# One attention and expert kernel: the product with v as 64-row products only, router work in smaller groups and other places, constants on another queue

## The chip, the cores and the metric

The kernel runs on one core of a Trainium2 chip. The metric is the device time of one execution in microseconds (us); lower is better. A profiled execution also leaves a trace, in which every instruction has its engine, its start and its length. The engines are PE (TensorE: matmuls; its weight loads are listed apart as PEld), DVE (VectorE), ACT (ScalarE), POOL (GpSimd) and SP (SyncE, which here only issues transfers). Each engine works through its own instructions in order.

## The reference

Two parts follow each other. The first is attention over a sliding window of 64 keys, for 8 batches, 8 heads, 576 positions and a head size of 64. The second routes each of the 4608 resulting rows of 512 numbers: a row whose skip score is not positive is left as it is, any other row goes through the one expert (of 8) with the highest logit and gets the weighted result added.

```python
scores = np.where(mask, scale * np.matmul(q, k.transpose(0, 1, 3, 2)), -1e9)   # mask: 0 <= rel < 64
attn = np.exp(scores - np.max(scores, axis=-1, keepdims=True))
attn = attn / (np.sum(attn, axis=-1, keepdims=True) + 1e-09)
x = np.matmul(attn, v)                       # then rows of 8 heads x 64 = 512
do_compute = x @ w_skip > 0
e_idx = np.argmax(xc @ w_gate, axis=1)       # xc: the rows that compute
h = np.maximum(xc[mask] @ w1[e], 0.0)
y[mask] = gate_w[mask, None] * (h @ w2[e])
out[do_compute] = xc + y
```

All data are float32.

## The kernel before

**Tiles.** The rows are cut into blocks of 64 positions, and two blocks make a token tile of 128 rows; there are 36 tiles, 0 to 35. Since the window is 64 wide, a block needs its own keys ("now") and those of the block before it. In most tiles the two blocks follow each other in one batch, so the keys and values of the first block are also the "before" block of the second. Tiles 8, 17, 26 and 35 are tail tiles: they hold the ninth blocks of two batches and share nothing. In tiles 0, 4, 9, 13, 18, 22, 27 and 31 the first block opens a batch and has no block before it.

**The attention loop.** The instructions are issued in a written-out order. Iteration t of the loop does this: `score(t + 1)` multiplies q with k on PE (16 matmuls into `ps`); the gate step of this tile, if there is one, on PE and ACT (`gate` multiplies vT with the router weights into `pw`, copied to `vw`; `gate_t` turns that round into `pk`, copied into nine extra columns of `vm`, so that the product with v yields the router's logits too); `transpose_p(t)` transposes the softmax numerators `s` on PE into `pt`, and ACT copies (`pm`) and POOL and DVE multiply with a mask to give `ptm`; `soften(t + 1)` takes the masked scores (DVE, `ps`), the maximum (DVE, `mx`), and the exponentials (ACT, `nmx` and eight instructions into `s`); `tile_out(t - 1)` calls `av_tile`, which multiplies `ptm` with v on PE into `av` and lets DVE divide by the row sums (`r`, `x`, `lh`).

**The product with v.** `av_tile` has two forms. In a tail tile every product has 64 rows of keys and 64 columns of queries: for each of four head pairs q, two windows, two blocks and two heads z. In the other tiles the block that both need is multiplied once for both, with 128 query columns (the part `(0, 2, 1, ...)` of the list `parts`), and the two other products have 64 columns. The trace has two records for each such matmul.

**The buffers.** `pt`, `pw` and `pk` take turns in two PSUM buffers (tag "t"); `ps` has two; `av` has one.

**The router.** `GRP` cuts the tiles into groups; when the last tile of a group is done, the generator `route` is queued, and `routes(1)` runs one step of it (a step is up to a `yield`) on DVE. Its matmuls (`sums`) go into the free end of `av`. Each row then gets a place in an expert's list, and POOL writes the list entries with indirect transfers, one per tile (`scatter`), which `pace` issues one or two at a time. After tile 21 (`NCLOSE` = 22 tiles) the two fullest experts are found (`close_first`), their lists are read back (`first_lists`), and their rows fetched (`gather_x`, indirect transfers `xg<-out,es`), so that the first expert can start while the last tiles are worked on. `split` transposes these rows on PE (`px`) in the iterations of `XSPLIT`; `U0` are the iterations in which SP issues the first six weight loads (`raw`), `USPLIT` that of the first split of weights. For 17 < t < 30 (set by `TWICE`) ACT and POOL do half of `ptm` and DVE the other half; otherwise ACT and POOL do three quarters. From iteration `TWICE` on two scatters are issued per iteration.

**The experts.** When the tiles are done, PE works through the experts' matmuls in `float32r` halves (`p`, `yw`, `yv`, `yu`), for which ACT and DVE split each weight piece in two (`whi`, `wlo`).

**Transfers.** q, k, vT, vm and the stores of x are issued by SP in order, and each new transfer on SP or ACT waits until the eighth before it has landed. They are spread over the tiles by `feed`, four or five tiles ahead of their use. The constants are issued by ACT; `load_constants` (the router's tables and the emptying of the lists) stands at the end of the opening loads.

## Time and profile before

| | before |
|---|---|
| median of 3 runs | 497.98 us (493.5 to 498.54) |
| the profiled execution | 500.87 us, of which the span from first to last instruction is 499.2 us |
| PE, DVE, ACT, POOL busy | 451.2, 283.0, 211.3, 178.5 us |
| mean granted TensorE clock | 0.934 |
| attention on PE (first to last product with v) | 20.0 to 231.9 us |

The page of the profile gives the busy time of each engine over the whole span and, in 40 slices, its share in tenths. [...] The chain of waits is followed back from the last instruction: at each step it names what released the work, so its rows in the attention show which engine set the pace there.

### The profile page before, as it was taken

To read this page: it belongs to the slowest core of one execution; us is meant where nothing else is said; L and a number is where in the kernel's file an instruction comes from. 1 tells how busy PE (TensorE), PEld (TensorE's weight loads), DVE (VectorE), ACT (ScalarE), POOL (GpSimd) and SP (SyncE) were. 2 spreads that over 40 slices of the span, in tenths; PEclk is the share of its full clock that TensorE was granted. 3 is DMA by queue.
4 is the path that set the end of the run, shared out by engine and by line. 5 is a ranking of instruction groups with operands and counts; after the bars stand their busy time and mean duration, and the time that the engine had idled before them with its cause. 6 is when DMAs were issued, how large, how long until landed. Compare 5 with 4: busy or idle time off the path is not lost.

```text
span 499.2 us, 12731 instructions
## 1 busy us (share of the span) xinstructions
PE 451.2 (90%) x5001; PEld 365.7 (73%) x5001; DVE 283.0 (57%) x600; ACT 211.3 (42%) x604; POOL 178.5 (36%) x213
## 2 busy tenths in 40 slices
PE   3999999899988994988798999999999999999990
PEld 3677767666765773767797988898888889888770
DVE  2356665665666664457963364967437456666420
ACT  1665665444434452334731252443424435543410
POOL 4343443344644546336525351420604313101010
PEclk9999999898977897668899999999999999999996
DMA  8879998868877698316743455364645655656000
GB/s 306 334 226 298 301 298 256 313 176 275 224 257 213 181 356 301 110 44 201 260 121 142 165 186 167 121 245 149 205 161 173 204 180 183 224 194 207 3 26 18
DMA packets 34958, 99.90 MB, mean 200 GB/s; under 512 B 6092, under 2 KB 7910, under 8 KB 34888
## 3 DMA queue, kind: packets, MB, share of 16 engines
q1 hardware_dynamic: 28864, 88.52, 54.5%
q0 software_dynamic: 4864, 9.90, 5.9%
q8 instruction: 40, 0.66, 0.5%
q10 hardware_dynamic: 1168, 0.65, 0.4%
q14 instruction: 22, 0.18, 0.1%
HBM read 84.82 MB, written 14.94 MB: 200 GB/s over the span
## 4 chain that ended last, share of the span: by engine, by line
PE 76%; DVE 8%; DMA 6%; issue 3%; ACT 3%; another core or an unknown queue 0%; POOLq 0%; SPq 0%; ACTq 0%; DVEq 0%
PE av L376 17%; PE p L750 7%; PE p L751 7%; PE p L752 7%; PE ps L244 5%; PE pt L276 5%; PE yw L750 3%; PE yv L750 3%; PE yw L751 3%; PE yv L751 3%; PE yw L752 3%; PE yv L752 3%; DMA raw<-wq 3%; PE px L739 2%; PE pk L339 2%
## 5 line engine op out<-in xcount | busy, mean ns | idle before, releaser
L376 PE MATMUL av<-vm,ptm 64*64 64x74 f32 (+1 forms) x1536 | 101.5, 285 | 1.9 <-DVE lh L394 1.5
L703 DVE TENSOR_TENSOR wlo<-raw,whi 128x1024 fp32r<-128x1024 f32 x72 | 87.8, 1222 | 14.3 <-ACT whi L702 12.4
L376 PEld LDWEIGHTS av<-vm,ptm 64*64 64x64 f32 (+1 forms) x1536 | 75.2, 164 | 27.6 <-issue 9.3
L787 ACT ACTIVATE hh<-p 128x256 fp32r<-128x256 f32 (+6 forms) x72 | 27.7, 385 | 140.6 <-PE p L752 139.2
L750 PE MATMUL p<-xh,whi 128*128 128x256 f32 (+6 forms) x288 | 85.8, 298 | 1.1 <-DVE hl L788 1.1
L751 PE MATMUL p<-xl,whi 128*128 128x256 f32 (+6 forms) x288 | 84.7, 294 | 0.0
L752 PE MATMUL p<-xh,wlo 128*128 128x256 f32 (+6 forms) x288 | 84.5, 293 | 0.0
L702 ACT CAST whi<-raw 128x1024 fp32r<-128x1024 f32 x72 | 74.5, 1046 | 0.0
L284 POOL TENSOR_TENSOR ptm<-pm,mask 128x512 f32<-128x512 f32 x36 | 45.9, 1276 | 76.1 <-ACT pm L283 76.0
L788 DVE SCALAR_TENSOR_TENSOR hl<-p,hh 128x256 fp32r<-128x256 f32 (+6 forms) x72 | 30.3, 420 | 70.3 <-ACT hh L787 64.6
L267 ACT ACTIVATE s<-ps,nmx 128x64 f32<-128x64 f32 x288 | 63.0, 330 | 1.2
L810 POOL DMA_INDIRECT out<-yo,les x18 | 19.0, 1054 | 122.3 <-DVE yo L809 109.8
L750 PEld LDWEIGHTS p<-xh,whi 128*128 128x128 f32 x288 | 55.7, 193 | 4.0 <-DVE hl L788 1.2
L528 POOL DMA_INDIRECT lists<-ent,gdi x36 | 40.7, 1130 | 46.4 <-DVE lh L394 22.6
L751 PEld LDWEIGHTS p<-xl,whi 128*128 128x128 f32 x288 | 55.8, 194 | 1.4
L752 PEld LDWEIGHTS p<-xh,wlo 128*128 128x128 f32 x288 | 55.7, 194 | 0.0
L276 PE MATMUL pt<-ident,s 128*128 128x128 f32 x144 | 34.5, 328 | 13.1 <-ACT vw L328 6.3
L386 DVE TENSOR_SCALAR r<-av 128x8 f32<-128x8 f32 x36 | 6.0, 166 | 71.1 <-PE av L376 69.4
L244 PE MATMUL ps<-k,q 64*64 64x128 f32 (+1 forms) x1024 | 42.7, 295 | 0.8 <-issue 0.8
L276 PEld LDWEIGHTS pt<-ident,s 128*128 128x128 f32 x144 | 16.3, 153 | 30.7 <-ACT vw L328 11.3
L244 PEld LDWEIGHTS ps<-k,q 64*64 64x64 f32 x1024 | 34.8, 153 | 2.0 <-issue 1.8
L750 PE MATMUL yw<-whi,hh 128*128 128x512 f32 x80 | 32.3, 403 | 0.0
(171 smaller groups left out, 703.2 us busy)
## 6 DMA issues: line engine op xcount, KB each, us to landing
raw<-wq SPq DMA_DIRECT2D x72, 512.0 KB
vm<-vp SPq DMA_DIRECT2D x16, 592.0 KB
vT<-vT SPq DMA_DIRECT2D x16, 512.0 KB
out<-x SPq DMA_DIRECT2D x32, 256.0 KB
q<-qT SPq DMA_DIRECT2D x14, 512.0 KB
k<-kT SPq DMA_DIRECT2D x7, 640.0 KB
k<-kT SPq DMA_DIRECT2D x7, 512.0 KB
kt<-kT SPq DMA_DIRECT2D x8, 256.0 KB
```

What stands on the lines that cost most here:

```text
L244: nc.tensor.matmul(ps[64 * hf : 64 * hf + 64, z, p, 64 * w.start :], q[h, p], k[h, w, p], start=True, stop=True, skip_group_check=True,)
L267: nc.scalar.activation(s[:, q, z], cur[:, z, q], AF.Exp, bias=nmx[:, z, q : q + 1], scale=0.125)
L276: nc.tensor.transpose(pt[:, i], s[:, 2 * g + i].rearrange("p z c -> p (z c)"), ident)
L284: nc.gpsimd.tensor_tensor(part(0, 2), split(pm[:, 0:2], 2), kept(2), op=ALU.mult)
L376: nc.tensor.matmul(av[64 * f0 : 64 * f1, z, q * VW : (q + 1) * VW], ptm[h, q, j : j + f1 - f0], v[h, q], start=first, stop=not first or (f ...
L528: ins = nc.gpsimd.indirect_dma_start(out=lists, out_offset=bass.IndirectOffsetOnAxis(ap=di, axis=0), in_=ent.bitcast(I32), in_offset=None, ...
L702: nc.scalar.copy(hi, raw)
L703: nc.vector.tensor_tensor(lo, raw, hi.bitcast(F32), op=ALU.subtract)
L750: nc.tensor.matmul(o, lh, rh, start=first, stop=False)
L751: nc.tensor.matmul(o, lh, rl, start=False, stop=False)
L752: nc.tensor.matmul(o, ll, rh, start=False, stop=last)
L788: beat(nc.vector.scalar_tensor_tensor(hl[:, f], p1, 0.0, hh[:, f].bitcast(F32), op0=ALU.max, op1=ALU.subtract))
```

## The change

- `av_tile` has one form for all tiles, that of the tail tiles: for each head pair and window, 64 by 64 products of the two blocks and two heads. The 128-column product is gone; a full tile takes 32 matmuls in place of 24, a tile that opens a batch 24 in place of 16.
- The gate steps come after `transpose_p(t)` and no longer before it.
- The router groups are 8, 8, 6, 8, 4, 2 tiles in place of 14, 8, 8, 4, 2; the boundary at tile 22 stays.
- The three calls of `routes` per iteration stand after `soften` and the loads, after `masks`, and at the end. The first stood ahead of `soften`.
- `load_constants` is issued by SP in iteration 1; on ACT the order of the small constants differs, and an exponential of the tile of ones (scale 0) is run there ahead of the first softmax.
- `U0`, `USPLIT`, `XSPLIT` and `TWICE` are one iteration later.

```diff
-U0 = (28, 29, 30, 31, 32, 33)
-USPLIT = (34,)
+U0 = (29, 30, 31, 32, 33, 34)
+USPLIT = (35,)
-XSPLIT = (32, 33)
+XSPLIT = (33, 34)
-TWICE = 20
+TWICE = 21
...
     def load_constants():
-        nc.scalar.dma_start(cf, a["c_f"])
-        nc.scalar.dma_start(trib, a["c_tri"])
-        nc.scalar.dma_start(
+        nc.sync.dma_start(cf, a["c_f"])
+        nc.sync.dma_start(trib, a["c_tri"])
+        nc.sync.dma_start(
...
-        nc.gpsimd.memset(onesb, 1.0)
...
-        shared = win[0][0] is win[1][1]
         for q in range(4):
-            parts = [] if shared else [(hf, hf + 1, 2 * hf + 1, win[hf][0], True) for hf in range(2)]
-            if shared:
-                parts.append((0, 2, 1, win[0][0], True))
-            parts += [
-                (0, 1, 0, win[0][1], False),
-                (1, 2, 3 if shared else 2, win[1][0] if shared else win[1][1], False),
-            ]
...
+            for w in range(2):
+                for hf in range(2):
+                    if win[hf][w] is None:
+                        continue
+                    for z in range(2):
+                        h = slice(64 * z, 64 * z + 64)
+                        nc.tensor.matmul(
+                            av[64 * hf : 64 * hf + 64, z, q * VW : (q + 1) * VW],
+                            ptm[h, q, 2 * hf + 1 - w],
+                            win[hf][w][h, q],
...
-    GRP = [14, 8, 8, 4, 2]
+    GRP = [8, 8, 6, 8, 4, 2]
...
         load_qk(0, 0, 2)
+        nc.scalar.dma_start(band, a["c_band"])
         nc.scalar.dma_start(identb, a["c_identb"])
-        nc.scalar.dma_start(band, a["c_band"])
         nc.scalar.dma_start(sel, a["c_sel"])
+        nc.scalar.dma_start(wg, a["wg"])
         nc.scalar.dma_start(ident, a["c_ident"])
         nc.scalar.dma_start(mask, a["c_mask"])
-        nc.scalar.dma_start(wg, a["wg"])
+        nc.gpsimd.memset(onesb, 1.0)
+        nc.scalar.activation(onesb, onesb, AF.Exp, scale=0.0)
...
-        load_constants()
...
             score(t + 1)
+            masks = transpose_p(t)
             for f, n in gate_at.get(t, ()):
                 f(n)
-            masks = transpose_p(t)
             rest = its[0].split(*xhl[0], XSPLIT.index(t), "t") if t in XSPLIT else None
-            routes(1)
             soften(t + 1)
             pace(1)
             feed(t, 0)
+            if t == 1:
+                load_constants()
+            routes(1)
             masks()
+            routes(1)
...
-            routes(1)
             routes(1 if t < NCLOSE - 1 else 2)
```

In iteration 5 PE's order before is this (`ps` are the scores of tile 6, `pk` a gate step, `pt` the transposes of tile 5, `av` the product of tile 4 or 5 with v; the line numbers of the changed kernel are up to 8 lower):

```order
L244 MATMUL ps<-k_109,q 64x128 x16
L339 MATMUL pk<-ident,vw_470 64x64 x8
L276 MATMUL pt<-ident,s 128x128 x4
L376 MATMUL av<-vm,ptm 128x74 x2
L376 MATMUL av<-vm,ptm 64x74 x4
L376 MATMUL av<-vm,ptm 128x74 x2
L376 MATMUL av<-vm,ptm 64x74 x4
L376 MATMUL av<-vm,ptm 128x74 x2
L376 MATMUL av<-vm,ptm 64x74 x4
L376 MATMUL av<-vm,ptm 128x74 x2
L376 MATMUL av<-vm,ptm 64x74 x4
```

and now this:

```order
L243 MATMUL ps<-k_109,q 64x128 x16
L275 MATMUL pt<-ident,s 128x128 x4
L338 MATMUL pk<-ident,vw_499 64x64 x8
L368 MATMUL av<-vm,ptm 64x74 x32
L243 MATMUL ps<-k_110,q 64x128 x16
L275 MATMUL pt<-ident,s 128x128 x4
```

The gate step has moved behind the transposes, and 24 products of two widths have become 32 of one.

At the same place ACT's order (the copies of the gate step and of the transposes, then the exponentials of the next tile) was

```order
L328 COPY vw_470<-pw 128x256
L283 COPY pm<-pt 128x256
L287 COPY pm<-pt 128x128
L264 ACTIVATE nmx<-mx 128x8
L267 ACTIVATE s<-ps,nmx 128x64 x8
```

and is

```order
L282 COPY pm<-pt 128x256
L286 COPY pm<-pt 128x128
L327 COPY vw_499<-pw 128x256
L263 ACTIVATE nmx<-mx 128x8
L266 ACTIVATE s<-ps,nmx 128x64 x8
```

The copy of the gate step now stands between the copies of the transposes and the exponentials.

On DVE the first router group began, before, like this (`lg` to `gfm` are router steps, `ps` and `mx` the next tile's softmax, `ptm` the masks):

```order
L394 TENSOR_TENSOR lh<-av,r 128x8x9
L421 TENSOR_REDUCE lg<-lh 128x126
L428 TENSOR_REDUCE gmx<-lg 128x14
L430 TENSOR_TENSOR gd<-lg,gmx 128x112
L433 SCALAR_TENSOR_TENSOR gfi<-gd,cf 128x112
L435 TENSOR_REDUCE gfm<-gfi 128x14
L260 COPY_PREDICATED ps<-sel,ps 128x8x64
L263 TENSOR_REDUCE mx<-ps 128x8
L291 TENSOR_TENSOR ptm<-pt,mask 128x256
```

and now, six tiles earlier in the program, it begins like this:

```order
L386 TENSOR_TENSOR lh<-av,r 128x8x9
L413 TENSOR_REDUCE lg<-lh 128x72
L259 COPY_PREDICATED ps<-sel,ps 128x8x64
L262 TENSOR_REDUCE mx<-ps 128x8
L420 TENSOR_REDUCE gmx<-lg 128x8
L422 TENSOR_TENSOR gd<-lg,gmx 128x64
L290 TENSOR_TENSOR ptm<-pt,mask 128x256
L425 SCALAR_TENSOR_TENSOR gfi<-gd,cf 128x64
L427 TENSOR_REDUCE gfm<-gfi 128x8
L378 TENSOR_SCALAR r<-av 128x8
```

One router step is left ahead of the next tile's softmax; the others stand behind its maximum and behind the masks.

## Rows read from the trace of the kernel before

**Rows 1.** The page: busy time of each engine, the granted clock in 40 slices, and the shares of the chain of waits by engine.

```profile
PE 451.2 (90%) x5001; PEld 365.7 (73%) x5001; DVE 283.0 (57%) x600; ACT 211.3 (42%) x604; POOL 178.5 (36%) x213
...
PEclk9999999898977897668899999999999999999996
...
PE 76%; DVE 8%; DMA 6%; issue 3%; ACT 3%; another core or an unknown queue 0%; POOLq 0%; SPq 0%; ACTq 0%; DVEq 0%
```

**Rows 2.** The chain of waits in order of time, pieces of the attention (start in us, length in us, what). 20.03 is the product of tile 0, 44.61 of tile 5, 59.40 of tail tile 8, 83.43 of tile 13, 176.14 of tile 28, 231.23 the end of tile 35's.

```profile
20.03 2.71 PE av L376 x30
...
44.61 2.66 PE av L376 x48
47.27 0.87 PE ps L244 x32
48.89 0.44 PE pt L276 x2
49.32 2.66 PE av L376 x48
...
59.40 1.19 PE av L376 x64
...
83.43 2.54 PE av L376 x30
...
176.14 2.71 PE av L376 x48
...
231.23 0.63 PE av L376 x19
```

**Rows 3.** Groups by line with the shapes kept apart, the product with v: shape of the loaded weights, operand, count of records, busy us and mean ns of one, idle time before.

```profile
L376 PE MATMUL av<-vm,ptm 64*128 64x74 f32 x512 | 62.9, 326 | 1.6 <-DVE lh L394 1.5
L376 PE MATMUL av<-vm,ptm 64*64 64x74 f32 x1024 | 54.3, 264 | 0.3 <-issue 0.3
```

**Rows 4.** The timeline behind tail tile 8: the gate step's matmuls and copy, then the copies, the maximum's scaling and the eight exponentials of ACT (start, length, engine, line; in brackets idle time ahead and what ended it).

```profile
62.20 0.64 PE L326 MATMUL pw<-vT,wg 128*32 128x256 f32 x8
...
62.91 0.37 ACT L328 COPY vw<-pw 128x256 f32<-128x256 f32 x1 [0.93 <-PE pw L326]
...
63.30 0.37 ACT L283 COPY pm<-pt 128x256 f32<-128x256 f32 x1
...
63.81 0.27 ACT L287 COPY pm<-pt 128x128 f32<-128x128 f32 x1
63.98 0.21 ACT L264 ACTIVATE nmx<-mx 128x8 f32<-128x8 f32 x1
...
64.22 1.75 ACT L267 ACTIVATE s<-ps,nmx 128x64 f32<-128x64 f32 x8
```

**Rows 5.** Busy time of each engine by stretch: the stretch, its length, then busy us of PE, PEld, DVE, ACT and POOL with the count of instructions, the granted clock, the share of the DMA engines and GB/s. The stretch from 20 to 84 us is tiles 0 to 13, that from 180 to 232 us the last tiles, that from 232 to 270 us the start of the experts.

```profile
20.00:84.00 64.00, 62.69 (x1235) 46.28 (x1234) 38.16 (x92) 38.13 (x159) 25.97 (x27) 1.00 0.88 277
45.00:57.00 12.00, 11.87 (x235) 8.63 (x239) 6.32 (x16) 7.80 (x34) 5.58 (x6) 1.00 0.96 321
63.00:69.00 6.00, 5.87 (x100) 4.39 (x98) 3.61 (x10) 3.71 (x15) 2.32 (x3) 1.00 0.97 351
...
180.00:232.00 52.00, 41.99 (x595) 32.29 (x587) 27.34 (x73) 20.96 (x73) 24.96 (x28) 0.74 0.55 190
232.00:270.00 38.00, 32.51 (x215) 29.76 (x215) 27.89 (x75) 16.35 (x27) 17.44 (x23) 0.96 0.60 196
```

**Rows 6.** The timeline of the opening: tile 0's maximum on DVE, ACT's issue of the emptying of the lists, and tile 0's exponentials.

```profile
7.70 0.69 DVE L263 TENSOR_REDUCE mx<-ps 128x8 f32<-128x512 f32 x1
...
9.48 1.27 ACTq L160 DMA_DIRECT2D lists<-c_list  x1
...
12.31 1.75 ACT L267 ACTIVATE s<-ps,nmx 128x64 f32<-128x64 f32 x8
```

**Rows 7.** The first router group: three pieces of the chain of waits from 87 to 100 us (start, length, what).

```profile
87.45 1.21 DVE lg L421
...
90.70 0.61 DVE ps L260
...
95.36 4.28 PE av L376 x48
```

**Rows 8.** The stretch behind it, columns as in rows 5.

```profile
95.40:102.20 6.80, 6.80 (x90) 4.75 (x90) 2.56 (x12) 1.95 (x9) 1.73 (x4) 0.50 0.74 270
```

**Rows 9.** The timeline of PE, the second pair of tile 19's transposes (in brackets idle time ahead and what ended it).

```profile
113.28 0.44 PE L276 MATMUL pt<-ident,s 128*128 128x128 f32 x2 [1.74 <-ACT vw L328]
```

**Rows 10.** The timeline of POOL: the last scatter of the second router group, and the first read of the early lists.

```profile
175.44 0.99 POOL L528 DMA_INDIRECT lists<-ent,gdi  x1 [1.39 <-DVE lh L394]
...
182.91 0.64 POOL L618 DMA_DIRECT2D es<-lists  x1 [5.17 <-DMA lists<-ent,gdi]
```

**Rows 11.** The chain of waits: the transfer of the first expert's rows (start, length, what).

```profile
191.51 6.00 DMA xg<-out,es
```

**Rows 12.** The timeline of PE: the transposes of these rows.

```profile
197.65 1.09 PE L739 MATMUL px<-ident,xg 128*128 128x128 f32 x4 [5.76 <-DMA xg<-out,es]
```

**Rows 13.** The timeline of PE in a stretch at the lower clock level: scores, a gate step and the transposes of one tile.

```profile
162.29 1.93 PE L244 MATMUL ps<-k,q 64*64 64x128 f32 x32
...
164.00 1.08 PE L339 MATMUL pk<-ident,vw 64*64 64x64 f32 x16
...
165.01 1.47 PE L276 MATMUL pt<-ident,s 128*128 128x128 f32 x4
```

## The prediction

> **What bounds the kernel now.** I read the page first: PE is busy for 90% of the span, no other engine for more than 57%, and the chain of waits runs through PE for 76% of the span [rows 1]. So a saving on PE should show, if nothing stands close behind it. I then followed the chain through the attention. From tile 0 to tile 13 it is PE almost without a break: scores 0.87 us, a gate step, transposes 0.44, the product with v 2.66, and the next tile again [rows 2]. The period is (83.43 - 20.03) / 13 = 4.88 us. From tile 13 to tile 28 it is (176.14 - 83.43) / 15 = 6.18 us, and the last seven tiles, into which the first expert's first matmuls are mixed, take from 176.14 to 231.86, 55.7 us [rows 2]. So the attention has 1.3 us per tile in its middle, and much more at its end, that are not PE's own work at full clock.

> What these extra times are: in the first router group five steps stand on DVE ahead of the next tile's softmax, from 87.45 to 90.70, 3.25 us in which PE runs dry; then PE gets half the clock for 6.8 us and a product takes 4.28 us in place of 2.66 [rows 7, 8]. Single stalls come on top, like 1.74 us in tile 19 [rows 9]. At the end the transposes of the first expert's rows wait 5.76 us for their transfer, and the mean granted clock from 180 to 232 us is 0.74 [rows 5, 12].

> The key row is the one tail tile on the chain. It already has the form that the change gives to all: 64 records of 64 by 64 in 1.19 us, while a full tile takes 2.66 us for 48 records [rows 2]. The sum of the single records hides this (264 and 326 ns each [rows 3]), since records in different corners of the array run beside each other; only start to end tells the price. In the full tiles two widths take turns.

> **The change part by part.**

> *Product with v.* 24 full tiles go from 2.66 to 1.19 us, 1.47 less. The 8 tiles that open a batch get 48 records: 1.19 x 48/64 = 0.89 against about 2.55, 1.66 less. Together 24 x 1.47 + 8 x 1.66 = 48.6 us of PE time, an upper bound of the gain at full clock. [...] The trace says 64 records in 1.19 us, 19 ns each, weight loads included [rows 2]. [...]

> *What is late next.* A full tile leaves PE 4.88 - 1.47 = 3.41 us of work. Per tile, of some 64 / 4.88 = 13.1 in the stretch from 20 to 84 us, DVE and ACT have 38.2 / 13.1 = 2.9 us each and POOL 2.0 [rows 5]. The gate step behind the transposes makes a ring on ACT: its matmuls need the `pt` buffer that the first `pm` copy frees, and its own copy stands ahead of the exponentials. From the end of one tile's exponentials: 0.37 (`pm`), 0.71 (start of the gate's matmuls to its copy), 0.37 (copy), 0.21 (`nmx`), 1.75 (exponentials) = 3.41 us, with hand-overs about 3.6 [rows 4]; the other `pm` copy lies inside the 0.71. Last the transfers: 277 GB/s x 64 us / 13.1 = 1.35 MB per tile [rows 5]. The two stretches with nearly full DMA engines (0.96 and 0.97) moved 321 and 351 GB/s, so a tile needs 4.2 or 3.85 us. I take the longer stretch: **4.2 us per tile, set by transfers**, with 3.6 (the ring) and 4.5 (300 GB/s, worse than either row) as ends.

> *Tiles 0 to 13.* 13 x (4.88 - 4.2) = 8.8 us. Two things come off: tile 8 has two gate steps, and the second waits for the second `pt` buffer until DVE's masks are done, about 1 us in series (0.64 and 0.37 [rows 4]); and the router group of 8 now falls here, in tiles 9 to 13. Its first five steps cost 3.25 x 8/14 = 1.9 us by the group of 14 [rows 7], all of it about twice that; DVE has 4.2 - 2.9 = 1.3 us free per tile, so I charge 1 us. Left: 7 us (ends 3 and 13).

> *Tiles 13 to 28.* Before 92.7 us, of which 15 x 4.88 = 73.2 are the plain period and 19.5 extra. With one router step ahead of the softmax in place of three, DVE's share of the extra shrinks, and with it the fall of the clock behind it; the stalls of other origin stay, and there are three groups in place of two up to tile 22, with about one more set of small DVE steps. I keep half, 10 us, and the period of 4.2: 63 + 10 = 73, a gain of 20 us (ends 8 and 29).

> *Last tiles.* Before 55.7 us, 7 x 4.88 = 34.2 plain and 21.5 extra. The chain of the early lists takes from the last scatter at 175.44 over the read at 182.91 to the end of the row transfer at 197.51, 22 us of waits for transfers [rows 10, 11]. It doesn't get shorter with PE. There were four iterations between the last scatter and the transposes; now there are five (`XSPLIT` is later, the scatter is not), 5 x 4.2 = 21 us: the wait of 5.76 us should shrink to 1 or 2. But POOL itself waits 5.17 us for the scatters, with the next masks queued behind, and a shorter tile hides less of it; I leave 17 of the 21.5. 7 x 4.2 + 17 = 46.4, a gain of 9 us (ends 0 and 17).

> *Opening.* Tile 0's maximum is ready at 8.39 us, but ACT begins the exponentials at 12.31: it still issues three constants [rows 6] and loads its table. These issues go to SP, where they stand in iteration 1 behind the loads of five tiles; the exponential of ones loads the table early. That is up to 3.9 us for the softmax, but the first values and their gate step still have to arrive and the array is slow there. I take 2 (ends 0 and 3.9). On SP the three issues hold up loads that are four or five tiles ahead; nothing, and at worst the 1.27 us of the longest [rows 6].

> *Experts.* From 232 us on nothing in PE's order changes. `U0` and `USPLIT` move by one iteration, which is now shorter. DVE is busy 27.9 of the 38 us there [rows 5]: 0, with 3 us either way.

> **Sum:** 2 + 7 + 20 + 9 = 38 us. The profiled execution took 500.9 us (span 499.2), so it would be 463; the median of the runs lies 2.9 us lower, 498 - 38 = **460 us**.

> **The rivals.**

> *The transfers give it back* (20%): the loads are squeezed into less time, the tile takes 4.5 us, and the three waits of the early lists, which share the DMA engines, grow by a third, 7 us. Gain 13 x 0.38 - 2 = 3 in the first tiles, 16 in the middle, 2 at the end, 2 in the opening, less than 1 of it lost elsewhere: about 22, so 476 us. For it: 0.96 and 0.97 of the DMA engines already busy in places. Against: 0.88 on average from 20 to 84 us, and loads four or five tiles ahead [rows 5].

> *The extra goes too* (8%): 351 GB/s are held, and the router no longer stops PE. The upper ends, 13 + 29 + 12 + 3, are 57 us: 441 us.

> *The clock falls in every tile: slower* (7%). [...] At that level a tile costs 1.93 (scores) + 1.08 (gate step) + 0.88 (transposes, twice 0.44; the row has 1.47) + 2.4 (product, twice 1.19) = 6.3 us [rows 2, 13]. The mean passes 4.88 once a third of the tiles runs so (4.2 + 2.1 x 1/3 = 4.9). With half of them it is 5.25, 35 x 0.37 = 13 us more than before: 511 us. Against it: behind tail tile 8, with its short product, the clock stayed at 1.00 up to 84 us [rows 2, 5], and it fell where PE had been empty for much longer than 0.8 us [rows 7, 8].

> *Number binds, not width* (2%): if a record costs what it costs in a full tile now, 2.66 / 48 = 55 ns, then 64 of them take 3.55 us, and 24 tiles x 0.89 give 21 us more: 519 us. [...] Against it stands the 1.19 us of the tail tile [rows 2].

> *The change doesn't do what it says* (5%): in a tail tile each block of v belongs to one product, in a full tile two products read the same block at once. If that or the shared `av` banks hold the product near 2.66 us, the rest is small moves: 497 us. Against it: 1.19 us was for the same banks and the same order of corners.

> **How the numbers follow.** The forecast keeps 58%: 460, from 448 to 472. Faster by over 1% (5 us, about what a measurement of this kernel can tell from no change) are the forecast and the first two rivals, 0.86; within 1% the last, 0.05; slower the clock and the number, 0.09. The range reaches from 443, inside the better case, to 484, past the rival of the transfers by the loosest of its terms; outside lie half of the better case, the unchanged time, the two slower ones and a little of the rest, about 0.2.

> **What would show it.** Right: a full tile's product at about 1.2 us from start to end, products 4 to 4.4 us apart up to tile 13 with ACT, DVE and transfers in the chain where PE was, DMA near full, tile 13's product near 74 us, tile 28's near 147, and the experts as long as before. Wrong: products still over 2 us; a granted clock below 1 before tile 13; a wait for the rows of the first expert as long as before or longer; or an expert part that starts earlier and ends no sooner.

## The result

| | before | changed | ratio, 95% interval |
|---|---|---|---|
| median, first set | 496.56 us (4 runs, 493.5 to 498.54) | 480.08 us (4 runs, 477.54 to 480.32) | 0.9662 [0.9596, 0.9727] |
| set beside `routes_old2` | 496.43 us | 479.24 us | 0.972 [0.96, 0.9839] |
| set beside `two_fix` | 498.63 us | 478.12 us | 0.9638 [0.9578, 0.9698] |

The changed kernel is faster, by 16.5 us where 38 were forecast. The forecast of 460 us was too low, and the measured time lies inside the range. The profiled executions have spans of 499.2 us before and 478.7 after, 20.5 apart. Slow runs, some 1.5% or more above a kernel's fastest, are left out of the ratios, and the profiled runs of the kernel before (500.87 us) and of `av_only` below (480.05 us) are slow ones.

The page of the changed kernel (busy time, granted clock in 40 slices as PEclk in tenths of full speed, the queues, the shares of the chain by engine) answers to [rows 1]:

```profile
PE 406.8 (85%) x5514; PEld 337.3 (70%) x5514; DVE 285.8 (60%) x616; ACT 209.8 (44%) x607; POOL 177.0 (37%) x216
...
PEclk9998998879987977779999999999999999999996
...
q8 instruction: 44, 0.72, 0.6%
...
PE 64%; DVE 13%; issue 8%; DMA 5%; ACT 4%; POOL 2%; POOLq 0%; another core or an unknown queue 0%; ACTq 0%; DVEq 0%; SPq 0%
```

PE has lost 44 us of busy time, near the 48.6 that the product alone was to give. But "issue" (time in which the engine waited for nothing that the profile shows) has gone from 3% of the chain to 8%, and a clock below 0.9 now also stands in two of the first seven slices, where there was none. The windows of four stretches, columns as in [rows 5]; they are tiles 0 to 13, 13 to 28, the last tiles and the start of the experts:

```profile
16.00:80.00 64.00, 50.13 (x1435) 38.99 (x1427) 41.74 (x106) 36.48 (x158) 29.18 (x34) 0.95 0.91 307
80.00:159.00 79.00, 60.86 (x1644) 46.88 (x1636) 57.34 (x158) 40.17 (x173) 40.88 (x42) 0.87 0.84 267
159.00:210.00 51.00, 36.83 (x798) 29.60 (x801) 29.57 (x75) 22.40 (x83) 25.01 (x28) 0.80 0.64 225
210.00:268.00 58.00, 52.01 (x355) 46.99 (x346) 34.34 (x89) 22.74 (x40) 23.70 (x38) 0.97 0.53 169
```

Read from the starts of the products with v (16.38 us for tile 0, 80.21 for tile 13, 159.37 for tile 28, and 210.32 for the end of the last), the gain came like this:

| piece | before, us | after, us | gain | forecast (ends) |
|---|---|---|---|---|
| up to tile 0's product | 19.96 | 16.38 | 3.6 | 2 (0 to 3.9) |
| tiles 0 to 13 | 63.40 | 63.83 | -0.4 | 7 (3 to 13) |
| tiles 13 to 28 | 92.71 | 79.16 | 13.5 | 20 (8 to 29) |
| tile 28 to the last product's end | 55.8 | 50.9 | 4.9 | 9 (0 to 17) |
| behind it | 267.3 | 268.4 | -1.1 | 0 (-3 to 3) |

The pieces add up to the 20.5 us between the two profiles, 4 more than the medians give.

**Where it went.** In the first tiles PE is empty for 14 of 64 us and the gain is nil. The chain of waits through tile 5's product, and through the scores after tile 15's (start, length, what), shows one kind of loss:

```profile
37.74 0.83 PE av L368 x45
38.57 2.76 issue
41.33 0.75 PE av L368 x11
...
89.95 0.23 PE ps L243 x10
90.18 4.16 issue
94.34 1.54 PE ps L243 x16
```

PE stops in the middle of a product, between two records that wait for nothing, and goes on 2.76 us later. The sums for PE by what it waited for, from 20 to 200 us (total, times, longest), put this first:

```profile
PE av L368 <- issue: 8.3, 8, 2.8
PE ps L243 <- issue: 8.2, 7, 4.2
PE av L368 <- POOL ptm L283: 5.6, 2, 4.1
PE pw L325 <- ACT pm L282: 4.2, 9, 2.0
```

In the kernel before, the same view has 0.8 us of it, in two waits:

```profile
PE ps L244 <- issue: 0.8, 2, 0.5
```

The longest one was there to be seen on PE's timeline, behind the short product of the first tail tile:

```profile
61.83 0.45 PE L244 MATMUL ps<-k,q 64*64 64x128 f32 x7 [0.50 <-issue]
```

The stops have a place in the instruction stream. I counted PE's recorded instructions (weight loads, matmuls and its waiting instructions) and set the packets of the instruction queue, q8, beside them. Each is 16 KB and takes 0.9 to 1.1 us, six of the 44 up to 2.3. That one packet is 256 instructions follows from the counts: 44 x 256 = 11264 beside 11234 recorded, and 40 x 256 = 10240 beside 10171 before. At four of the stops (times in us):

```
ahead of instruction   last start   first start   fetch (q8)
1473                   38.35        41.33         39.10 to 40.03
2753 = 1473 + 5*256    67.12        69.67         67.15 to 68.06
3009 = 2753 + 256      73.46        75.12         72.64 to 73.68
3777 = 3009 + 3*256    89.96        94.34         91.91 to 92.87
```

In three profiles (this one, `after_c` and `base_late` below) PE stood for more than 0.3 us at 37 such borders, and each time it went on 1.2 to 1.6 us behind the end of the last fetch. So PE's instructions come in blocks of 256, and the next block was not there yet. The 0.50 us of the kernel before lie at such a border too (instruction 1985 = 1473 + 2*256). Up to the end of the attention the stops, from start to start, add up to 17.7 us in this profile (32 borders, 10 stops over 0.3 us), 13.5 us of them before tile 16; in the kernel before, 1.4 us (27 borders).

Numbering the fetches and the blocks in order, a fetch starts on average 2.6 us after PE enters the block ahead of the one it brings (before: 2.2; up to 5.9 and 5.4). With 0.95 for itself and some 1.4 until PE goes on, a block must last about 5 us (an estimate, the sum of these three). From 30.00 to 88.30 us the kernel before used 2272 weight loads and matmuls, 256 in 6.6 us: almost no loss. At the changed kernel's undisturbed 3.4 to 3.6 us per tile and 219 to 220 instructions, 256 last 4.0 to 4.2 us.

After some of the stops the clock falls too. These are the 3.6 us behind the first stop above, the 3.4 us behind the one that ends at 69.67, where it stays at 1.00, and the 4.9 us behind the one that ends at 75.12, with the granted clock third from the end (before, this part of the program stood at 1.00 throughout [rows 5]):

```profile
41.40:45.00 3.60, 3.36 (x55) 2.78 (x59) 2.36 (x6) 0.49 (x2) 0.04 (x1) 0.58 1.05 378
70.00:73.40 3.40, 3.10 (x121) 2.69 (x111) 2.34 (x6) 0.77 (x4) 1.30 (x3) 1.00 0.86 311
75.10:80.00 4.90, 4.58 (x91) 3.72 (x90) 2.41 (x6) 1.35 (x6) 2.56 (x4) 0.65 0.77 202
```

**Two waits on POOL.** Its timeline answers to [rows 10]:

```profile
25.28 0.19 POOL L164 COPY base<-cf 128x8 f32<-128x8 f32 x1 [8.54 <-DMA cf<-c_f]
25.44 1.26 POOL L283 TENSOR_TENSOR ptm<-pm,mask 128x512 f32<-128x512 f32 x1
...
157.10 1.00 POOL L520 DMA_INDIRECT lists<-ent,gdi  x1 [0.17 <-DVE r L379]
164.69 0.60 POOL L610 DMA_DIRECT2D es<-lists  x1 [6.59 <-DMA lists<-ent,gdi]
...
166.48 1.27 POOL L283 TENSOR_TENSOR ptm<-pm,mask 128x512 f32<-128x512 f32 x1
```

The copy of `base` now waits for `cf`, which SP issues in iteration 1 behind the loads of several tiles; tile 2's masks are queued behind it, and its product comes 7.00 us after tile 1's. The read of the early lists waits 6.59 us for the scatters (5.17 before), and the masks behind it hold the next product for 4 us. On PE's timeline that product, and the transposes of the first expert's rows [rows 12], which no longer wait for their transfer:

```profile
167.81 1.02 PE L368 MATMUL av<-vm,ptm 64*64 64x74 f32 x24 [4.05 <-POOL ptm L283]
...
186.92 0.65 PE L731 MATMUL px<-ident,xg 128*128 128x128 f32 x4 [2.74 <-DVE ptm L290]
```

### The profile page after: what moved, and what is told of

It reads as the page before. It is cut to its first block, busy times and chain, and to the rows that moved or that the text cites. A ratio compares the mean times of both kernels' runs of the same rounds, so it can differ in the third digit from the quotient of the medians.

```text
span 478.7 us, 13812 instructions
## 1 busy us (share of the span) xinstructions
PE 406.8 (85%) x5514; PEld 337.3 (70%) x5514; DVE 285.8 (60%) x616; ACT 209.8 (44%) x607; POOL 177.0 (37%) x216
## 4 chain that ended last, share of the span: by engine, by line
PE 64%; DVE 13%; issue 8%; DMA 5%; ACT 4%; POOL 2%; POOLq 0%; another core or an unknown queue 0%; ACTq 0%; DVEq 0%; SPq 0%
PE av L368 8%; PE p L744 7%; PE p L742 7%; PE p L743 7%; PE ps L243 4%; PE yw L742 3%; PE yv L742 3%; PE yw L743 3%; PE yv L744 3%; PE yv L743 3%; PE yw L744 3%; DVE wlo L695 3%; PE pt L275 2%; ACT s L266 2%; PE px L731 2%
## 5 line engine op out<-in xcount | busy, mean ns | idle before, releaser
L779 ACT ACTIVATE hh<-p 128x256 fp32r<-128x256 f32 (+6 forms) x72 | 27.7, 385 | 140.0 <-PE p L744 135.7
L368 PE MATMUL av<-vm,ptm 64*64 64x74 f32 x2048 | 55.9, 248 | 15.5 <-issue 8.3
L368 PEld LDWEIGHTS av<-vm,ptm 64*64 64x64 f32 x2048 | 48.3, 149 | 22.6 <-issue 15.1
L520 POOL DMA_INDIRECT lists<-ent,gdi x36 | 38.2, 1062 | 48.8 <-DVE lh L386 15.0
L243 PE MATMUL ps<-k,q 64*64 64x128 f32 (+1 forms) x1024 | 46.0, 296 | 10.5 <-issue 8.2
L243 PEld LDWEIGHTS ps<-k,q 64*64 64x64 f32 x1024 | 36.5, 153 | 14.3 <-issue 12.6
L259 DVE COPY_PREDICATED ps<-sel,ps 128x512 f32<-128x512 int32 x36 | 25.4, 705 | 18.9 <-PE ps L243 8.6
L282 ACT COPY pm<-pt 128x256 f32<-128x256 f32 x36 | 13.6, 377 | 46.5 <-PE pt L275 41.3
```

The source lines that it names most:

```text
L243: nc.tensor.matmul(ps[64 * hf : 64 * hf + 64, z, p, 64 * w.start :], q[h, p], k[h, w, p], start=True, stop=True, skip_group_check=True,)
L368: nc.tensor.matmul(av[64 * hf : 64 * hf + 64, z, q * VW : (q + 1) * VW], ptm[h, q, 2 * hf + 1 - w], win[hf][w][h, q], start=w == 0, stop=w ...
L520: ins = nc.gpsimd.indirect_dma_start(out=lists, out_offset=bass.IndirectOffsetOnAxis(ap=di, axis=0), in_=ent.bitcast(I32), in_offset=None, ...
L779: nc.scalar.activation(hh[:, f], p1, AF.Relu)
```

## The experiments

Theory at the start: the blocks of PE's instructions come too late (delivery). Rivals: transfers set the pace, as forecast; PE's own time and clock; the POOL wait for `cf`. The kernels of one set ran on one chip; the kernel before had medians from 487 to 499 us over the sets, so ratios compare better than times.

### The parts alone

`av_only` is the kernel before with the new product with v and nothing else:

```diff
-        shared = win[0][0] is win[1][1]
...
+            for w in range(2):
+                for hf in range(2):
+                    if win[hf][w] is None:
+                        continue
```

> The kernel before with the new form of the product with v and nothing else. Theory 'delivery': PE now works faster than its instructions arrive (they come in blocks of 256, each by a transfer of 16 KB that is ordered one block ahead and waits among the loads), so the product falls to about 1.25 us but PE stands still 0.5 to 4 us at many block borders; the router steps still stand ahead of the softmax. 482 to 488 us. Theory 'the parts are independent': the product alone gives 16 of the 16.5 us, 480 us, and the other parts nothing. Theory 'transfers' (the forecast's: the loads set 4.2 us per tile): tiles evenly 4.2 us apart up to tile 13, without standstills at block borders, 470 to 476 us.

Measured 478.45 us, ratio 0.9787 [0.9582, 0.9992]. PE's waits from 20 to 200 us:

```profile
PE av L369 <- issue: 14.4, 9, 2.8
PE ps L244 <- issue: 10.4, 7, 2.7
PE pw L326 <- issue: 5.2, 2, 2.9
```

This one edit brings the stops, 30 us of them here, and a gain of 2.1%, with an interval that reaches nearly to none. `wide` is the other way round: the changed kernel with the old product.

> The changed kernel with the old product with v (128 columns for the shared block) put back; all other parts of the change stay. Delivery: PE sets the pace again with 4.8 us per tile in tiles 2 to 13, its blocks last over 6 us each and no standstill is over 1 us; the other parts bring only the opening and some router stalls, 488 to 495 us. If the other parts were what made the kernel faster: 482 us or less. If the gate steps behind the transposes cost PE time when PE sets the pace (about 0.3 us per tile): 497 to 505 us.

Measured 500.22 us, ratio 1.0306 [1.017, 1.0441]. The other parts alone are no gain but a loss of 3%, the third figure of the expectation: tiles 2 to 14 are 5.10 us apart, 4.85 in the kernel before. That the gate steps are its cause, as the expectation has it, was not tested with this product. With the old product no wait on "issue" is among PE's waits of over 0.15 us from 20 to 200 us, so the stops belong to the product's form. `base_late` moves the copy of `base` to iteration 6:

```diff
-        nc.gpsimd.tensor_copy(base, cf[:, off["base"]])
...
+            if t == 6:
+                nc.gpsimd.tensor_copy(base, cf[:, off["base"]])
```

> The changed kernel with POOL's copy of the list starts (it waits for the constants that SP now loads in iteration 1) moved from iteration 1 to iteration 6. Theory 'POOL': tile 2's masks no longer stand behind that wait of 8.5 us, the products of tiles 1 and 2 are 3.5 to 4 us apart in place of 7.0, and the whole is 3 us faster, 477 us. Theory 'transfers' or 'delivery catches up': the 3 us are lost again before tile 13, since the loads or the blocks come no sooner, 479 to 481 us.

Measured 474.12 us, ratio 0.980 [0.9675, 0.9925], beside 0.9787 for `av_only` in the same set: on top of the product, the other parts give nothing that can be told. I took the 474.12 us for a gain over the changed kernel, until both ran on one chip:

> The changed kernel with the POOL copy of base moved to the sixth iteration, beside the changed kernel on one chip for the first time. If the wait for cf (8.5 us on POOL, 3.4 us more between the products of tiles 1 and 2) is a loss of its own: 3 to 6 us faster than after_c. Rival: PE's later stops take it back, within 1 us of after_c.

478.12 us for the changed kernel and 480.51 for this one, 0.9638 [0.9578, 0.9698] and 0.9663 [0.9601, 0.9725]: no difference. Tile 2's product comes 1.2 us earlier, and tile 28's starts at 159.81 us in both. The rival held: the wait of 8.5 us on POOL costs nothing that can be told in the end.

The order of gates and transposes, and the router groups, each put back to the form of before on top of `base_late`:

> base_late with the gate steps ahead of the transposes of P again, as in the kernel before. Theory G (the order costs: behind the transposes, the copies of vw and vm stand behind pm on ACT and the masks wait less): the order of the change is right and this is slower by 2 to 6 us than base_late. Rival: with the gates behind, PE's pw and pk wait for ACT's pm copies, and putting them ahead gives back 0.2 to 0.4 us in each second tile, 3 to 8 us faster than base_late.

476.34 us, ratio 0.9524 [0.9463, 0.9584], beside 477.18 and 0.9554 [0.9472, 0.9636] for `base_late` in the same set: the same, and both figures expected were wrong.

> base_late with the router groups of the kernel before (14, 8, 8, 4 and 2 tiles) and its steps at the old places of the loop. Theory R (the new groups and places pay: no router step ahead of softmax, the last groups close earlier): 4 to 10 us slower than base_late (0.955 to 0.980 to before), most of it around the groups' ends at tiles 14 to 17 and in the last six tiles. Rival: the groups only move the stops, and PE's instruction blocks set the time: within 3 us of base_late.

481.62 us, ratio 0.9803 [0.9641, 0.9966], beside 479.24 and 0.972 [0.96, 0.9839] for the changed kernel: no difference that can be told. `base_late` itself did not run in this set.

### Transfers or instructions

`no_kv` leaves out the loads of k and vT from the fifth half batch on (v itself, in `vm`, still comes), so only the attention's times are to be read:

```diff
-                when_at(first_of[n] - AHEADQ, 0, load_k, n)
+                if n < 4:
+                    when_at(first_of[n] - AHEADQ, 0, load_k, n)
...
+        if n >= 4:
+            vms[n] = None, vts[n % 2]
+            return None
```

> As base_late, but the loads of k and of vT are left out from the fifth half batch on (the old contents are used again), so that about 13 of the 50 MB of the attention don't move; PE's instructions are the same. Only the attention is read. Delivery, with the blocks' transfers waiting among the loads: they start sooner behind a border (median about 1 us in place of 2.7), the sum of the standstills at block borders up to the end of the attention falls from about 17 us to under 6, and the last product ends 8 to 15 us sooner than in base_late. Delivery with a fixed time per block: standstills as before, and the end within 3 us. 'Transfers': tiles 25% closer together in the stretches without standstills too.

Tile 28's product starts at 150.99 us (`base_late`, same set, 153.56). From tile 2 to tile 14 the bytes fall by 31% (218 GB/s x 54.97 us against 297 x 58.41), the time per tile by 6%, from 4.87 to 4.58 us. Stops at block borders up to the end of the attention were 19.8 us (`base_late` 27.7), and the last product ends 5.0 us sooner (196.9 against 201.9): neither the 6 us of stops of the first theory nor tiles closer by 25% came. Even the 6% is within what one kernel's profiles differ by: three of `base_late` have 4.87, 4.90 and 5.21 us per tile, three of the changed kernel 4.79, 4.82 and 4.95. So bytes alone are not what holds the tiles. Then the number of instructions, up and down. `more_instr` adds 16 matmuls of one column per tile, 32 instructions:

```diff
+        for _ in range(16):
+            nc.tensor.matmul(
+                av[0:64, 0, 400:401], identb[0:64, 0:64], band[0:64, 0:1], start=True, stop=True, skip_group_check=True
+            )
```

> base_late with 16 matmuls of one bf16 column more in each tile's product with v (32 PE instructions more, into columns of the PSUM tile that nothing reads). Theory A (delivery): 36 tiles x 32 instructions are 4.5 blocks more, each block lasts shorter, and standstills of 1 to 2 us are added in most tiles: 484 to 500 us. Theory B (no limit by number): PE's own added time is about 1 us per tile and lies partly in its idle time, 474 to 484 us. In both the standstills stay at multiples of 256 instructions if the limit is the block, so they move to other places of the program than in base_late.

496.23 us, ratio 0.9892 [0.9807, 0.9977], 19 us over `base_late` of the same set (477.18), and stops of 28.7 us in place of 17.6. As delivery has it; but PE's own time per tile grew as well, so it is not yet proof. `two_groups` takes 32 instructions away by the 24 wide products, put in the order of their widths:

```diff
-        for q in range(4):
-            for w in range(2):
-                for hf in range(2):
...
+        for f0, f1, j, v, first in parts:
+            for q in range(4):
+                for z in range(2):
```

> base_late with the product with v as 24 instructions again where the middle block is shared, but all 8 of 64 rows x 128 columns first and then all 16 of 64x64, so that the tile shape changes about twice per tile and not after every product; 32 fewer PE instructions per full tile than with 32 products. Theory A (PE's instructions come too late: a block of 256 lasts 3.6 us at 32 products): the blocks last longer, the standstills at multiples of 256 become rarer or shorter, 458 to 468 us although a product may take 1.4 to 1.8 us. Theory B (the number of instructions does not matter, PE's own time does): the product gets longer by 0.2 to 0.5 us and the time stays or rises, 474 to 485 us.

In this order its sums are not the reference's, so the expert part works on other numbers, its 553.76 us say nothing, and only the attention counts. There the stops are nearly gone, 2.6 us in all; the product takes 2.11 us. With one start flag per bank:

> two_groups with one start flag for each PSUM bank in place of one for each head pair, so that the sums are those of the reference and the expert part can be compared; base copy late. By two_groups' attention (tile 13 at 77.1 us, 1 to 3 us ahead of the changed kernel, then 4 to 5 us behind it by tile 28, with standstills of 2.6 us in all): if what it lost in the middle came from the other numbers, 465 to 474 us; if it is PE's longer product (2.1 us in place of 1.3) in a stretch at the lower clock, 478 to 490 us.

488.49 us, ratio 0.9795 [0.9724, 0.9866]: 10 us slower than the changed kernel. Stops 3.0 us, tiles 2 to 14 at 4.88 us (changed kernel 4.95). PE is busy for 51.3 of the 58.5 us of these tiles, in the changed kernel for 47.3 of 59.3: what delivery gave up, PE's longer product took. The mixed kernels use the old product in every second or third tile:

```diff
+        if t % 2 == 1:
...
+        else:
```

> base_late with the 24 wide products of the kernel before in every second tile, and the 32 products of 64x64 in the others. Theory A (a block of 256 PE instructions must last about 5.0 us, since its successor's fetch starts on average 2.6 us after PE enters a block in base_late_b's attention, takes 0.95, and PE goes on some 1.4 us behind it): 216 instructions per tile and 3.42 and 4.9 us per tile in turn make 4.9 us per block, so PE almost never stands still and keeps its clock; the middle goes from 5.0 us per tile (base_late_b, tiles 2 to 28) to about 4.2 to 4.6: 455 to 472 us, faster than base_late although half the tiles use the slower product. Theory B (the time follows PE's own work): 18 tiles x 1.4 us of longer product come on top, 485 to 500 us.

> The same with the wide products in every third tile only. Theory A: 221 instructions per tile in 3.9 us make 4.5 us per block, so some standstills stay: between base_late and mixed2, 462 to 478 us. Theory B: 12 tiles x 1.4 us more than base_late, 482 to 494 us.

486.99 us, 0.9871 [0.961, 1.0132], and 483.7 us, 0.9782 [0.9588, 0.9975], beside 479.24 for the changed kernel. Theory A's times did not come. The stops did shrink as it has it, to 5.3 and 7.2 us (18 to 19 in the changed kernel), but `mixed2` still takes 5.08 us per tile from 2 to 14, at a clock of 0.92. So far stops had nearly vanished twice without a gain, each time with more PE work in their place (54.5 of 60.9 us busy in `mixed2`).

### Number against time

`half_av` keeps every transfer and the short form, and leaves out the products with the previous block (w = 1): 64 instructions fewer per full tile.

```diff
-            for w in range(2):
+            for w in range(1):
...
-                            stop=w == 1 or win[hf][1] is None,
+                            stop=True,
```

> base_late with the products with the previous block left out (w = 1), so 16 products of 64x64 per tile and 64 fewer PE instructions; all loads stay. The sums are not the reference's, so only the attention up to tile 28 is to be read. Three theories of what holds the tiles at 4.8 to 5.0 us on average between tiles 2 and 14: transfers (as the prediction had it) give 4.2 to 5.0 us per tile still, since every byte is still loaded; the delivery of PE's instructions (168 per tile, a block of 256 lasts 5.2 us at ACT's 3.42 us per tile, and 5.0 are needed) gives 3.4 to 3.8 us per tile with almost no standstill at multiples of 256; the clock alone (PE idles more, so it is lowered more often) gives 4.0 to 4.6 with low-clock stretches behind no stop.

Tiles 2 to 14 at 3.98 us, 4.26 from 2 to 28, and tile 28's product at 135.30 us, 24.5 us ahead of `after_c`, the changed kernel in the same set. No theory's figure came exactly: 3.98 lies between the 3.4 to 3.8 of delivery and the 4.0 and 4.2 at which the other two begin. Here number and PE time fell together. `half_long` gives most of the time back and not the number, by streaming twice the columns in 12 of the 16 products (the expectation says each, but those of the last head pair have no further columns and keep 74):

```diff
-                            av[64 * hf : 64 * hf + 64, z, q * VW : (q + 1) * VW],
+                            av[64 * hf : 64 * hf + 64, z, q * VW : min(q + 2, 4) * VW],
...
-                            win[hf][w][h, q],
+                            win[hf][w][h, q : min(q + 2, 4)],
```

> half_av (the products with the previous block left out, so only the attention up to tile 28 is to be read) with each of its 16 products streaming 148 columns of v in place of 74, the surplus overwritten by the next product: as many PE instructions as half_av, but a product of 1.1 to 1.6 us from start to end, near the 1.31 of the changed kernel. If PE's own time makes the tiles slow: back to 4.6 to 5.0 us per tile between tiles 2 and 14 (half_av 3.98). If the number of instructions does: 4.0 to 4.3 us, and standstills at multiples of 256 instructions of 2 to 7 us in all up to the end of the attention (half_av 4.6).

`half_more` gives the number back, by 32 matmuls of one column (as in `more_instr`), and keeps the short product. These three kernels ran once each, `half_av` in the set of `after_c` and the two others on another chip.

> half_av with 32 matmuls of one bf16 column more per tile, so that the count of PE instructions per tile is that of the changed kernel again, while the sums, the masks and the transfers are those of half_av; PE's own time per tile comes near the changed kernel's too. If the number of instructions makes the tiles slow: 4.7 to 5.1 us per tile between tiles 2 and 14, standstills at multiples of 256 of 15 to 25 us in all. If the transfers or the real product do: 4.0 to 4.3 us as half_av.

The windows from tile 2's product to tile 14's, one for each kernel, columns as above (the changed kernel in `after_c`, then `half_av`, `half_long`, `half_more`):

```profile
26.04:85.38 59.34, 47.33 (x1314) 36.84 (x1315) 37.05 (x98) 31.98 (x140) 29.94 (x33) 0.91 0.88 285
```

```profile
24.54:72.32 47.78, 40.64 (x982) 29.84 (x980) 37.75 (x101) 33.59 (x146) 28.41 (x32) 0.93 1.00 357
```

```profile
23.61:71.97 48.36, 41.67 (x984) 31.30 (x982) 37.19 (x101) 33.88 (x146) 28.22 (x32) 1.00 0.97 349
```

```profile
26.95:89.22 62.27, 53.82 (x1366) 44.27 (x1364) 37.23 (x99) 33.77 (x146) 28.43 (x33) 0.86 0.81 254
```

And `base_late`, `no_kv`, `more_instr` and `two_fix`:

```profile
24.34:82.75 58.41, 44.27 (x1320) 34.57 (x1317) 37.80 (x101) 33.41 (x146) 28.97 (x33) 0.97 0.91 297
```

```profile
24.39:79.36 54.97, 45.51 (x1318) 36.16 (x1317) 36.77 (x99) 33.85 (x146) 27.75 (x32) 0.94 0.67 218
```

```profile
26.54:90.98 64.44, 52.52 (x1511) 42.20 (x1509) 37.68 (x99) 33.66 (x146) 28.59 (x33) 0.91 0.81 258
```

```profile
24.48:83.02 58.54, 51.29 (x1145) 42.12 (x1141) 38.12 (x102) 33.49 (x146) 29.15 (x33) 0.97 0.94 304
```

Divided by 12 tiles, with the stops at block borders inside these windows:

| kernel | us per tile | PE instructions per tile | full tile's product, us | stops, us | clock | DMA |
|---|---|---|---|---|---|---|
| changed (`after_c`) | 4.95 | 219 | 1.31 | 10.0 | 0.91 | 0.88 |
| `base_late` | 4.87 | 220 | 1.31 | 12.7 | 0.97 | 0.91 |
| `no_kv` | 4.58 | 220 | 1.31 | 7.3 | 0.94 | 0.67 |
| `more_instr` | 5.37 | 252 | 1.31 and 16 small | 8.7 | 0.91 | 0.81 |
| `two_fix` | 4.88 | 190 | 2.11 | 1.2 | 0.97 | 0.94 |
| `half_av` | 3.98 | 164 | 0.80 | 2.7 | 0.93 | 1.00 |
| `half_long` | 4.03 | 164 | 1.16 | 5.5 | 1.00 | 0.97 |
| `half_more` | 5.19 | 228 | 0.80 and 32 small | 6.9 | 0.86 | 0.81 |

`half_long` has a product 0.15 us shorter than the changed kernel's, and `half_av` another 0.36 less: the tile goes from 4.95 to 4.03 with the first step, where the number falls, and to 3.98 with the second, where only time does. The first step is the one that counts, since both half kernels stand at the limit of the DMA engines (shares of 1.00 and 0.97). Of its 11.0 us over the 12 tiles, 5.3 are time that PE was empty, about 4 of it at block borders, and 5.7 are time that PE was busy, of which the product's 0.15 us make 1.8; the rest goes with the granted clock, 0.91 against 1.00. So in this short form it is mainly the number of PE instructions that makes the tiles long, by the stops and by a lower clock. Over the whole attention `half_long`'s stops came to 9.0 us, more than the 2 to 7 expected. `half_more` goes back up with the number, a little past the 4.7 to 5.1 us expected, its stops at the lower end of what was expected (15.0 us); its small matmuls also cost PE time (undisturbed tiles 3.93 us apart, `half_av` 3.12) and its clock fell further, so it points the same way without being clean. `two_fix`, like the kernel before, took in 39 PE instructions per us, the two half kernels at the DMA engines' limit 41, and the five with 219 or more per tile 44 to 48.

Tiles 2 to 14 of `half_av` and `half_long` also show what stands behind delivery: DMA engines at 1.00 and 0.97 with 357 and 349 GB/s, at 4.0 us per tile. That is the limit of the forecast, reached only here.

None of these kernels that give the reference's result is shown to beat the changed one.

## Why the prediction was wrong

**Product with v: right.** 1.26 to 1.31 us for a full tile at full clock, by start to end, where the tail tile had promised 1.19; 64 records in 1.31 us are 20 ns each.

**"4.2 us per tile, set by transfers": the step that failed.** Tiles 0 to 13 took 4.91 us each. Undisturbed tiles are 3.4 to 3.6 us apart, the lower end (ACT's ring), so transfers were not what came next; some of these tiles may live on loads that were already there. What came next was not in the list at all: with 219 to 220 instructions per tile, blocks of 256 have to follow each other in about 4 us and take about 5. The stops of over 0.3 us in these tiles add up to 8.4 us, beside the 13 x (4.91 - 4.2) = 9.2 us that were missed here. The limit by transfers is real, as `half_av` shows with 3.98 us at a DMA share of 1.00; it stands behind this one. The page of the kernel before held the two numbers that were needed, 40 packets and 0.66 MB on the instruction queue, and the trace one stop of 0.50 us behind the only product that already had the new form. I looked at that tile for its 1.19 us and gave its stop no price.

**"Nothing" for constants issued by SP.** The price was for SP's queue alone. The wait that it adds is on POOL, 8.54 us, with tile 2's masks behind it. It was missed, but it is not what was lost: without it the time is the same within the interval (`base_late_c`).

**Tiles 13 to 28.** 13.5 us in place of 20. The period term is wrong here as in the first tiles, with fewer stops (4.4 us ahead of tile 16 and 2.6 at 137 us are the long ones) and more waits for masks and copies behind router steps (2.0 us at 125, 2.1 at 143 us on PE). The mean clock was 0.87, 0.85 before. That a third as many router steps ahead of the softmax would give back 10 us was not seen: `routes_old2`, with the old steps and places, is not slower by more than noise.

**Last tiles.** 4.9 us in place of 9, inside its ends, by the mechanism named: POOL's wait for the scatters grew (6.59 us), and the masks behind it are no longer hidden. That the transposes of the expert rows would stop waiting for their transfer was right.

**Opening and experts** came out inside their ends, 3.6 and -1.1 us.

**The rivals.** Transfers giving it back (476 us) was nearest by its number and not by its cause. Its sum is also off: by its own terms the middle gives 92.7 - 15 x 4.5 - 10 = 15 us and the end 55.7 - 7 x 4.5 - 17 - 7 = 0.2, where it has 16 and 2, so the gain would be 20 us and the time 478. "The extra goes too" adds 12 and 3 as upper ends where the parts have 17 and 3.9, which would be 435 us. The clock did fall in the first tiles, but behind stops in which PE was empty for 1.4 to 2.8 us, not the 0.8 that a tile of 4.2 us leaves beside 3.4 of work, and not behind each of them. "Number binds" had 2% with a price per record; the number does bind, by blocks and not by record.

**What stays open.** The stops add up to 17 to 19 us in three profiles of the changed kernel, close to what is missing (21.5 us by the medians, 17.5 by the two profiles), and some of them take some clock with them (0.58 and 0.65 in the two windows above). But they can't simply be subtracted: other profiles, of `base_late` and `gates_first2`, have 27.7 and 33.0 us of stops at about the same time, and in `two_fix` and `mixed2` they shrank without a gain. How much of the missing gain is theirs stays open. And why a fetch starts 2 to 6 us late in the attention was not found; with 31% fewer bytes (`no_kv`) it was 2.2 us on average in place of 2.8, the 2.2 of the kernel before. That a fetch waits among the loads, as the delivery theory of `av_only` has it, was not shown.

## What to carry to other kernels

Before a product is cut into more and smaller matmuls, count PE's instructions per us, weight loads included, and not only their time: here, over 12 tiles, 39 per us were almost free of stops, and no kernel passed 48. A single short stop by "issue" in a stretch that already has the new form can be a price to be multiplied and not noise. And a move's waits are to be looked for on every engine that reads what is moved, though a wait that is found may still cost nothing if a slower limit follows.
